# One butterfly level ahead of a block inverse, and a new order of the first loads, in a convolution and FFN kernel

## The chip, the cores and the metric

The kernel runs on one core of a Trainium2 chip. Its engines work side by side, each through its own list of instructions in order: TensorE (PE, with its weight loads as PEld), VectorE (DVE), ScalarE (ACT), GpSimd (POOL) and SyncE (SP), which here issues nearly all DMAs. They meet at semaphores. The metric is the device time of one launch in microseconds (us). Six runs of the kernel before took 351.58 to 353.56 us, with a median of 353.37 us.

## The reference

Two layers, each run twice, over x of 2048 rows and 512 channels (bf16). Layer A is a long convolution with gates; layer B is a gated FFN of width 1792.

```python
def _A_ref(q, k, v, shift_k, ssm_k, ssm_D):          # S = 2048
    k_shift = sum of 4 shifted copies of k, each times a tap per channel
    kv = k_shift * v
    y = irfft(rfft(pad(kv, 2S)) * rfft(pad(ssm_k, 2S)))[:S].astype(bfloat16)
    y = y + kv * ssm_D
    return q * y
def _B_ref(x, w_gate, w_up, w_down):
    return (silu(x @ w_gate) * (x @ w_up)) @ w_down
x = A_q
x = x + _A_ref(layernorm(x), k, v, ...)
x = x + _B_ref(layernorm(x), ...)
x = x + _A_ref(layernorm(x), k, v, ...)
x = x + _B_ref(layernorm(x), ...)
```

The convolved sequence y doesn't depend on x, so it is computed once and used by both A layers. The term with ssm_D is folded into the filter's first row.

## The kernel before

**Tiling.** The 2048 rows are cut into four blocks of 512, and a block into four residues r of 128 rows (row 4p + r lies on partition p). The convolution is done by blocks in the frequency domain. A block's spectrum has four slots with a real and an imaginary part of 128x512 each. Forward transforms are matmuls with the tables `fwd` (14 blocks of 128x128), computed on the chip; inverse transforms use the tables `inv`, which are `fwd` transposed by two DMA transposes (L966). `G[j]` is the spectrum of filter block j, `X[i]` that of block i of k_shift * v; `product(i, j)` (L619) adds X[i] * G[j] into `Z[i + j]`, and an inverse turns Z[k] into `Y[k]`, four rows of 128x512.

**Stages.** The first block has a path of its own. `load_h`, `load_k`, `load_v`, `load_x` (L356 to L394) and `load_weights` bring in filter, k, v, q and the three weights. `transpose_h` (L471) turns the filter, `half` (L429) and `butterfly` (L441) make G[0], `transpose_k` and `shift_mul` make k_shift * v in v's buffer `vt`, `direct` (L454) makes X[0] by 32 matmuls without a butterfly, `product` is called slot by slot, and `inverse_direct` (L686) makes Y[0]. In `inverse_direct` every one of the four output rows sums over all four slots and both parts: 4 x 4 x 2 = 32 matmuls of 128x512 into four PSUM buffers, which ACT then copies to Y (L701). The later blocks use `inverse` (L673) instead: two butterfly levels on VectorE and 8 matmuls.

`prologue(0, 0, 0, True)` (L779) follows: the normalised rows n are multiplied by y and added to x (L797, L799), `ln_stats` (L704) takes the statistics of the new rows on VectorE and raises them to -1/2 on POOL (L714), `normalise` writes z (L764), TensorE transposes z into `ptz` (L811), and ACT copies that to zT (L813), which the first FFN unit multiplies with the weights. With `on_pe=False`, as in all later prologues, DMA transposes make zT.

`ffn` (L820) runs 16 units: four blocks, two layers, two halves of 256 rows. A unit has 14 column tiles of w_gate and of w_up in four groups (`GROUPS`); ACT evacuates both (L854, L858), VectorE multiplies them into ht (L861), and w_down is accumulated into `pd` (L874). In some units x is put into pd first, by a matmul with the identity (L833). Convolution work of later blocks, in `conv(c)`, is laid between the units' matmuls.

**Order.** A planner, the class `Plan`, writes out each engine's instructions. Every operation is added with an engine, a cost, the buffers it reads and writes and, if wished, a latency, a due time and operations that come before it (`after`). `dues` works due times back from those that follow, `forward` then simulates the engines and takes, on each, the ready operation by start and due time. Rings such as "pf" (four PSUM buffers), "pd" and "pc" (two each), "v" (one buffer) and "ks" (two) say how many buffers rotate. The constants at the head of the file (`T0`, `DUR`, `STRETCH`, `SLK`) feed the due times only. On the chip an instruction waits for the data and buffers it uses, not for what `after` names. Eight semaphores serve the DMAs in turn, so that a DMA also waits for the eighth before it.

The lines that set SyncE's order of the first loads:

```python
    k0 = load_k(0, -69)
    v0 = load_v(0, -59, after=[k0])
    x0 = load_x(0, -58, after=[v0])
    wg = load_weights("g", -57, after=[x0])
    for n in range(2):
        ...
        tabs = add("SP", 2.2, ... dma_start_transpose(out=inv.t[:, sl, :], ...), due=-56.8, after=[wg])
    load_h(1, "SP", -56.5, after=[tabs])
    load_k(1, -56.4, after=[tabs])
    load_weights("u", -56, after=[tabs])
    load_weights("d", -55, after=[tabs])
```

Block 1's v, added later as `v1 = load_v(1, ...)`, takes the one buffer of ring "v" that block 0 used. Its product with k_shift is on VectorE too (L513), out of the copies ks that ACT makes (L512).

Of the kernel before, what the change touches and what calls it, by code (L numbers as in the profile page):

```python
# [19 lines left out]
SLK = 25.89  # L20
# [3 lines left out]
ASL = -144.04  # L24
# [4 lines left out]
HSL = 57.15  # L29
# [3 lines left out]
TINY = 0.2  # L33
Z_DUE = -45
X_PE = lambda l, c, h: (l, c, h) in {(0, 0, 0), (1, 2, 0)}
RINGS = {}
T0, FLOOR = 48.85, 3.32
DUR = [32.03, 59.44, 73.66, 74.27, 18.69, 11.93, 40.53, 46.32, 9.45, 36.19, 57.12, 39.57, 69.48, 86.77, 41.93, 24.18]
STRETCH = {1: {'PE': 13.87, 'DVE': 6.22, 'ACT': 7.89, 'POOL': 860.46, 'SP': 1855.74}, 2: {'PE': 5.7, 'DVE': 2.02, 'ACT': 0.72, 'POOL': 0.5, 'SP': 3.41}, 3: {'PE': 16.83, 'DVE': 2.04, 'ACT': 0.66, 'POOL': 0.59, 'SP': 6.47}}
# [26 lines left out]
class Plan:  # L66
# [50 lines left out]
    def dues(self, stretch, floor, units, back):  # L117

        nxt = {}
        for o in reversed(self.ops):  # L120
            d = 1e9 if o.fixed is None else o.fixed
            if isinstance(d, tuple):
                unit, share, shift, kind = d
                d = units[unit][0] + share * units[unit][1] + shift - back.get(kind, 0.0)
            for s in o.succs:
                d = min(d, s.due - o.cost - self.gap(o, s, s.preds[o]))
            if o.conv:
                d = min(d, nxt.get(o.eng, 1e9) - o.cost * stretch[o.grp][o.eng])
                nxt[o.eng] = d
                d = max(d, floor)  # L130
            o.due = d - o.sl

# [138 lines left out]
def kernel(  # L271
# [84 lines left out]
    def load_h(b, eng="SP", due=None, after=()):  # L356
        hn[b] = new("s8" if b == 1 else "h", "hn", [P, KD, L], parts=1)
        q = nc.sync if eng == "SP" else nc.scalar
        return add(eng, 0.55, lambda: q.dma_start(out=hn[b].t[:], in_=h3[:, :, b * L:(b + 1) * L]), w=[hn[b]], lat=(3.9, 10.0)[b] if b < 2 else 6.0, due=due, after=after)

    def load_k(b, due=None, after=()):
        if b == 0:
            kn[b] = new("s8", "kn", [P, R, D])
            return add("SP", 0.5, lambda: nc.sync.dma_start(out=kn[b].t[:], in_=k_t[:, b]), w=[kn[b]], lat=3.9, due=due)
        kT[b] = new("s8" if b == 1 else "k", "kTb", [P, KD, PADL + L])
        add("SP", 2.2, lambda: nc.sync.dma_start_transpose(out=kT[b].t[:], in_=k3[b * L - PADL:(b + 1) * L]),
            w=[kT[b]], lat=12.0 if b == 1 else 8.0, due=due, after=after)

    def transpose_k(b, ring, engs):
# [3 lines left out]
        for dt in range(KD):  # L373
# [5 lines left out]
            add("PE", pe(R, P), go, r=[kn[b], ident], w=[pt])  # L379
# [4 lines left out]
            else:  # L384
                add("DVE", tt1(D), lambda src=src, dst=dst: nc.vector.tensor_copy(out=dst(), in_=src()), r=[pt],
                    w=[(kT[b], (dt,))])

    def load_v(b, due=None, after=()):
        vt[b] = new("v", "vt", [P, R, D], parts=R)
        return add("SP", 0.6, lambda: nc.sync.dma_start(out=vt[b].t[:], in_=v_t[:, b]), w=[vt[b]], lat=4.5 if b else 5.3, due=due, after=after)  # L390

    def load_x(c, due=None, after=()):
        xs[c] = new("x", "xc", [P, R, D], parts=R + 2)
        return add("SP", 0.7, lambda: nc.sync.dma_start(out=xs[c].t[:], in_=q_t[:, c]), w=[xs[c]], lat=4.5 if c else 6.3, due=due, after=after)  # L394
# [17 lines left out]
    def spectrum(name):  # L412
        return new("s8", name, [P, 4, 2, D], parts=8)
# [105 lines left out]
    def by_residue(rows, ev, scale, ring, engs, conv):  # L519

        for r in range(R):
            for part, f in enumerate(("C", "nS")):
                ps = new(ring, "ps", [P, D], F32)
                add("PE", pe(1), lambda ps=ps, f=f, r=r: mm(ps.t[:], [(fT(f, r), rows.t[:, r, :])]),
                    r=[(rows, (r,)), fwd], w=[ps], conv=conv, dest=ev)
# [160 lines left out]
    def inverse_direct(k, slots_order):  # L686
# [13 lines left out]
        for r in range(R):  # L700
            add("ACT", act(D), lambda r=r: nc.scalar.copy(out=y.t[:, r, :], in_=pss[r].t[:]), r=[pss[r]], w=[(y, (r,))])  # L701


    def ln_stats(c, rows):  # L704
# [9 lines left out]
        add("POOL", PW, lambda: nc.gpsimd.tensor_tensor(out=rstd.t[:], in0=ve.t[:], in1=nhalf.t[:].to_broadcast((P, n)),  # L714
# [64 lines left out]
    def prologue(layer, c, h, on_pe=False):  # L779
# [16 lines left out]
        for o, i in enumerate(rows):  # L796
            dve(D, lambda o=o, i=i: nc.vector.tensor_mul(out=n.t[:, o, :], in0=n.t[:, o, :], in1=y.t[:, i, :]),  # L797
                [(y, (i,))], [(n, (o,))])
            dve(D, lambda o=o, i=i: nc.vector.tensor_add(out=x.t[:, i, :], in0=x.t[:, i, :], in1=n.t[:, o, :]),  # L799
                [(n, (o,))], [(x, (i,))])  # L800
        st = ln_stats(c, rows)
        stats = plan.ops[-2]
        done = []
        for o, i in enumerate(rows):
# [8 lines left out]
            add("ACT", act(D), lambda pt=pt, o=o: nc.scalar.copy(out=zT.t[:, :, o, :], in_=pt.t[:]), r=[pt], w=[(zT, (o,))], due=Z_DUE)  # L813
# [149 lines left out]
    wg = load_weights("g", -57, after=[x0])  # L963
    for n in range(2):
        sl = slice(n * NI, (n + 1) * NI)
        tabs = add("SP", 2.2, lambda sl=sl: nc.sync.dma_start_transpose(  # L966
            out=inv.t[:, sl, :], in_=fwd.t[:, sl, :].rearrange("p k f -> p (k f)")), r=[fwd], w=[(inv, (n,))], lat=8.0, due=-56.8,
            after=[wg])
    load_h(1, "SP", -56.5, after=[tabs])
    load_k(1, -56.4, after=[tabs])  # L970
    load_weights("u", -56, after=[tabs])
    load_weights("d", -55, after=[tabs])
    hs = transpose_h(0, "pf", (0, 2, 1, 3), False, ("DVE", "ACT"), drow)
    ev = spectrum("ev")
    G[0] = H[0] = spectrum("G0")
    half(hs, ev, "ac", 2.0 / N, "pf", ("ACT", "DVE"), False, -60)
# [20 lines left out]
    transpose_k(0, "pc", ("ACT", "DVE"))  # L997
    shift_mul(0, "pf", False, due=-49)
    normed[0, 0, 0] = apply_norm(0, 0, on_act=True, due=-47)
    butterfly(ev, G[0], 0, False)  # L1000
    X[0] = spectrum("X0")
    direct(vt[0], X[0], "pf", ("ACT", "ACT"), (0,))
    half(hs, ev, "bd", 2.0 / N, "pf", ("ACT", "ACT"), False)
    butterfly(ev, G[0], 1, False)
    direct(vt[0], X[0], "pf", ("ACT", "ACT"), (2, 1, 3))
# [6 lines left out]
    inverse_direct(0, (0, 2, 1, 3))  # L1012
# [89 lines left out]
```

## Time and profile before

| what | value |
|---|---|
| profiled execution, whole | 351.21 us |
| its span, first to last instruction | 349.4 us |
| granted TensorE clock | 1.00 |
| median of six runs | 353.37 us |
| L697, inverse matmuls of 128x512 | 32 |
| first and last start of L697 | 19.6 and 41.2 us |
| z L764, first start | 34.27 us |
| first FFN matmul (pf, L334) | 36.83 us |
| v of block 1: issue, time to landing | 21.74, 11.7 us |

The profile's rows read as follows. A row of the groups or the timeline has the engine, the line of the source, the operation, the buffer written and those read, and the shape; "x4" counts instructions. In the chain of waits each step is what released the one after it, or what stood before it on its engine, so it leads back from the last instruction. In the rows by stretch the busy us of each engine stand with the number of instructions in brackets, then the granted clock, the mean busy share of the 16 DMA engines, which can pass 1 where packets overlap, and GB/s. Times count from the start of the span. A few per cent of the matmul records are missing in the trace, so their counts run a little short.

### The profile page before, as it was taken

The page shows a single profiled execution, that of the slowest core. Times are in us where ns is not written, and L with a number is a line of the kernel's source. Part 1 is how long each engine was busy: PE and PEld are TensorE (multiplying, and loading weights), DVE is VectorE, ACT ScalarE, POOL GpSimd, SP SyncE. Part 2 cuts the span into 40 slices and gives each one's busy share as a digit, 9 for nine tenths or more (in the row PEclk, how much of TensorE's full clock was granted, in tenths as well). Part 3 has the DMA queues.
Part 4 walks back from the last instruction along what each step waited for, and adds up shares of the span by engine and source line. Part 5 has one row for each costly group of instructions (what it writes and reads, how often), then busy time and mean ns, then how long its engine had stood idle before and what let it go on. Part 6 is the DMA issues. An engine that isn't in the chain of part 4 may idle for free.

```text
span 349.4 us, 6596 instructions
## 1 busy us (share of the span) xinstructions
PE 339.9 (97%) x2597; PEld 249.0 (71%) x2625; DVE 276.6 (79%) x466; ACT 259.0 (74%) x508; POOL 38.1 (11%) x46
## 2 busy tenths in 40 slices
PE   7997999999999999999999999999999999999996
PEld 6655876858588685858586777758586877777684
DVE  6885989999998997899999999999997523643120
ACT  6986996757779994938896989859983756548460
POOL 4100010211120100201212001101001000100000
PEclk9999999999999999999999999999999999999999
DMA  7999211010152106320113030120101110000201
GB/s 255 307 331 350 52 60 32 0 32 0 34 118 64 30 13 141 101 51 2 31 33 76 17 102 20 38 54 0 33 30 28 35 32 0 17 17 1 62 0 30
DMA packets 42073, 22.96 MB, mean 66 GB/s; under 512 B 33845, under 2 KB 39866, under 8 KB 42042
## 3 DMA queue, kind: packets, MB, share of 16 engines
q1 hardware_dynamic: 41370, 21.95, 23.8%
q10 hardware_dynamic: 672, 0.59, 0.6%
q8 instruction: 20, 0.33, 0.4%
q14 instruction: 11, 0.09, 0.1%
HBM read 12.33 MB, written 2.10 MB: 41 GB/s over the span
## 4 chain that ended last, share of the span: by engine, by line
PE 77%; DVE 14%; DMA 5%; ACT 2%; issue 1%; DVEq 0%
PE pf L334 46%; PE pd L874 23%; PE ps L334 5%; DMA vt<-in_A_v_dram 3%; PE ps L462 2%; DVE ht L861 2%; DVE bnst L709 1%; DVE t L649 1%; DMA hn<-in_A_ssm_k_dram 1%; DVE t L657 1%; DVE t L645 1%; DVE Z L659 1%; DVE ka L600 1%; DVE Z L654 1%; DVE m L532 1%
## 5 line engine op out<-in xcount | busy, mean ns | idle before, releaser
L334 PE MATMUL pf<-zT,wg_sb 128*128 128x256 bf16 x896 | 116.1, 273 | 0.2
L334 PE MATMUL pf<-zT,wu_sb 128*128 128x256 bf16 x896 | 116.1, 273 | 0.1
L334 PEld LDWEIGHTS <-wg_sb 128*128 128x128 bf16 x896 | 87.5, 98 | 17.5 <-issue 1.1
L874 PE MATMUL pd<-wd_sb,ht 128*128 128x512 bf16 (+1 forms) x445 | 97.8, 372 | 1.1 <-issue 0.2
L334 PEld LDWEIGHTS <-wu_sb 128*128 128x128 bf16 x896 | 87.7, 98 | 13.0 <-issue 0.2
L854 ACT ACTIVATE sg<-pf 128x512 bf16<-128x512 f32 x112 | 67.6, 605 | 15.6 <-PE pf L334 14.1
L874 PEld LDWEIGHTS <-ht 128*128 128x128 bf16 x462 | 44.9, 98 | 48.0 <-DVE ht L861 1.2
L858 ACT CAST ht<-pf 128x512 bf16<-128x512 f32 x112 | 66.1, 590 | 15.0 <-PE pf L334 14.3
L861 DVE TENSOR_TENSOR ht<-ht,sg 128x1024 bf16<-128x1024 bf16 (+1 forms) x64 | 39.3, 618 | 24.8 <-ACT ht L858 24.8
L714 POOL TENSOR_TENSOR rstd<-ve,nhalf 128x2 f32<-128x2 f32 x24 | 26.2, 1093 | 215.4 <-DVE ve L712 206.2
L910 ACT CAST dn<-pd 128x512 bf16<-128x512 f32 x26 | 14.1, 597 | 35.0 <-PE pd L874 35.0
L709 DVE BATCH_NORM_STATS2 bnst<-xc 128x6 f32<-128x512 bf16 x48 | 31.0, 685 | 0.7
L913 DVE TENSOR_TENSOR xc<-xc,dn 128x1024 bf16<-128x1024 bf16 x13 | 8.9, 687 | 17.1 <-ACT dn L910 17.1
L645 DVE TENSOR_TENSOR t<-X,G 128x2048 bf16<-128x2048 bf16 x18 | 21.9, 1217 | 0.1
L649 DVE TENSOR_TENSOR t<-X,G 128x2048 bf16<-128x2048 bf16 x18 | 21.9, 1216 | 0.0
L423 ACT ACTIVATE X<-ps 128x512 bf16<-128x512 f32 x32 | 18.2, 613 | 0.2 <-PE ps L462 0.2
L659 DVE TENSOR_TENSOR Z<-Z,t 128x2048 bf16<-128x2048 bf16 x12 | 14.7, 1222 | 0.2
L657 DVE TENSOR_TENSOR t<-t,t 128x2048 bf16<-128x2048 bf16 x12 | 14.7, 1221 | 0.2
L740 POOL TENSOR_TENSOR rstd<-ve,nhalf 128x2 f32<-128x2 f32 x8 | 7.6, 956 | 64.2 <-ACT ve L738 64.2
L786 DVE TENSOR_TENSOR n<-n,Yk 128x1024 bf16<-128x1024 bf16 x15 | 10.3, 690 | 5.4 <-ACT n L759 4.1
L423 ACT ACTIVATE H<-ps 128x512 bf16<-128x512 f32 x24 | 12.9, 610 | 2.1 <-PE ps L334 2.1
L734 ACT ACTIVATE jk<-xc,nm 128x512 bf16<-128x512 bf16 x16 | 11.5, 721 | 0.3
(105 smaller groups left out, 319.3 us busy)
## 6 DMA issues: line engine op xcount, KB each, us to landing
vt<-in_A_v_dram SPq DMA_DIRECT2D x4, 512.0 KB, 6.6
xc<-in_A_q_dram SPq DMA_DIRECT2D x4, 512.0 KB, 7.4
out_dram<-xc SPq DMA_DIRECT2D x15, 128.0 KB, 1.8
wg_sb<-in_B_w_gate_dram SPq DMA_DIRECT2D x1, 1792.0 KB, 12.3
wu_sb<-in_B_w_up_dram SPq DMA_DIRECT2D x1, 1792.0 KB, 7.8
wd_sb<-in_B_w_down_dram SPq DMA_DIRECT2D x1, 1792.0 KB, 13.6
hn<-in_A_ssm_k_dram SPq DMA_DIRECT2D x3, 512.0 KB, 7.2
hn<-in_A_ssm_k_dram ACTq DMA_DIRECT2D x1, 512.0 KB, 4.1
```

The source lines that it names most:

```text
L334: nc.tensor.matmul(o, lhsT=lhsT, rhs=rhs, start=(n == 0), stop=(n == len(terms) - 1))
L423: add("ACT", act(D), lambda: nc.scalar.activation(out=view(), in_=ps.t[:], func=ACT.Copy, scale=scale), r=[ps], w=[(buf, keys)], conv=conv)
L645: dve(n * D, lambda t1=t1, part=part: nc.vector.tensor_mul(out=t1.t[:], in0=x.t[:, sl, 0, :], in1=g.t[:, sl, part, :]), [(x, key(slots, (0 ...
L649: dve(n * D, lambda t2=t2, part=part: nc.vector.tensor_mul(out=t2.t[:], in0=x.t[:, sl, 1, :], in1=g.t[:, sl, 1 - part, :]), [(x, key(slots ...
L657: dve(n * D, lambda t1=t1, t2=t2, comb=comb: nc.vector.tensor_tensor(out=t1.t[:], in0=t1.t[:], in1=t2.t[:], op=comb), [t2], [t1], conv=conv)
L659: dve(n * D, lambda t1=t1, part=part: nc.vector.tensor_add(out=z.t[:, sl, part, :], in0=z.t[:, sl, part, :], in1=t1.t[:]), [t1], [zk], con ...
L709: add("DVE", 0.6, lambda st=st, i=i: nc.vector.bn_stats(out=st.t[:], in_=xs[c].t[:, i, :]), r=[(xs[c], (i,))], w=[st])
L714: add("POOL", PW, lambda: nc.gpsimd.tensor_tensor(out=rstd.t[:], in0=ve.t[:], in1=nhalf.t[:].to_broadcast((P, n)), op=ALU.pow), r=[ve, nha ...
L854: add("ACT", act(D), lambda ps=ps, o=o, sg=sg: nc.scalar.activation(out=sg.t[:, o:o + 2, :], in_=ps.t[:], func=ACT.Silu), r=[ps], w=[(sg, ...
L858: add("ACT", act(D), lambda ps=ps, o=o, ht=ht: nc.scalar.copy(out=ht.t[:, o:o + 2, :], in_=ps.t[:]), r=[ps], w=[(ht, (o // 2,))], due=(uni ...
L861: dve(n * W, lambda sg=sg, ht=ht: nc.vector.tensor_mul(out=ht.t[:], in0=ht.t[:], in1=sg.t[:]), [sg], [ht], due=(unit, k / pairs, 0.0, "h"))
L874: nc.tensor.matmul((pds[o] if not cs.start else pds[HP]).t[:, cs], lhsT=ht.t[:, q, o * P:(o + 1) * P], rhs=wt["d"].t[:, ft, cs], start=(ft ...
```

## The change

Block 0's inverse is made by a new function `inverse_half`. VectorE forms sums and differences of the slots s and s + 2 (four operations of 128x1024), and each output row then sums over two slots and two parts: 16 matmuls of 128x512 in place of 32. Row 0 of y is not copied to SBUF before its first use: VectorE multiplies straight from PSUM, and ACT copies the row for later use. In that prologue the second row's zT is evacuated on VectorE instead of ACT.

The load of filter block 1 is put ahead of w_gate. The two table transposes get, besides w_gate, the first transposes of k0 as predecessor in the planner, and are added after them. The planner's estimates of several loads and many due-time constants change, and 27 operations get an extra shift of their due time (`SHIFTS`). `X0` and `H0` select the paths that the kernel before had ("direct", "half"); only `I0` selects a new one.

```diff
-SLK = 25.89
+SLK = 25.57
-ASL = -144.04
+ASL = -167.89
-HSL = 57.15
+HSL = 49.11
+SHIFTS = {8: -168.0, 9: -2.0, 32: -48.0, 36: -20.0, 48: -11.0, ... }
+X0, H0, I0 = 'direct', 'half', 'half'
-T0, FLOOR = 48.85, 3.32
+T0, FLOOR = 25.95, -54.39
...
+        for n, d in SHIFTS.items():
+            self.ops[n].due += d
...
-        return add(eng, 0.55, ..., lat=(3.9, 10.0)[b] if b < 2 else 6.0, due=due, after=after)
+        return add(eng, 0.55, ..., lat=(3.9, 8.0)[b] if b < 2 else 6.0, due=due, after=after)
...
-            add("PE", pe(R, P), go, r=[kn[b], ident], w=[pt])
+            o = add("PE", pe(R, P), go, r=[kn[b], ident], w=[pt])
+            k_in = o if dt == 0 else k_in
...
-        for r in range(R):
+        fresh[k] = pss
+        evacuate_y(k, range(1, R))
+    def evacuate_y(k, rows):
+        y, pss = Y[k], fresh[k]
+        for r in rows:
             add("ACT", act(D), lambda r=r: nc.scalar.copy(out=y.t[:, r, :], in_=pss[r].t[:]), r=[pss[r]], w=[(y, (r,))])
+    def inverse_half(k, pairs):
+        y, z = new_y(k), Z[k]
+        m = spectrum("m")
+        pss = [new(("pd", "pd", "pf", "pf")[r], "ps", [P, D], F32) for r in range(R)]
+        count = [0] * R
+        for s in pairs:
+            for slot, op in ((s, ALU.add), (s + 2, ALU.subtract)):
+                dve(2 * D, lambda s=s, slot=slot, op=op: nc.vector.tensor_tensor(
+                    out=m.t[:, slot], in0=z.t[:, s], in1=z.t[:, s + 2], op=op), ...)
+            for r in range(R) if s == pairs[-1] else (0, 2, 1, 3):
+                for part in (0, 1):
+                    f, q, slot = next((f, q, t) for f, q, t, pt in INV_TERMS[r] if t % 2 == s and pt == part)
+                    count[r] += 1
+                    add("PE", pe(1), ... nc.tensor.matmul(pss[r].t[:], lhsT=iT(f, q), rhs=m.t[:, slot, part], ...),
+                        r=[(m, (2 * slot + part,)), inv], w=[pss[r]])
+        fresh[k] = pss
+        evacuate_y(k, range(1, R))
...
-            dve(D, lambda o=o, i=i: nc.vector.tensor_mul(out=n.t[:, o, :], in0=n.t[:, o, :], in1=y.t[:, i, :]),
-                [(y, (i,))], [(n, (o,))])
+            if i == 0:
+                ps = fresh[c][0]
+                dve(D, lambda: nc.vector.tensor_mul(out=n.t[:, 0, :], in0=n.t[:, 0, :], in1=ps.t[:]), [ps], [(n, (0,))], one=True)
+                evacuate_y(c, (0,))
+            else:
+                dve(D, lambda o=o, i=i: nc.vector.tensor_mul(out=n.t[:, o, :], in0=n.t[:, o, :], in1=y.t[:, i, :]),
+                    [(y, (i,))], [(n, (o,))])
...
-            add("ACT", act(D), lambda pt=pt, o=o: nc.scalar.copy(out=zT.t[:, :, o, :], in_=pt.t[:]), ...)
+            if o:
+                add("DVE", tt1(D), lambda pt=pt, o=o: nc.vector.tensor_copy(out=zT.t[:, :, o, :], in_=pt.t[:]), ...)
+            else:
+                add("ACT", act(D), lambda pt=pt, o=o: nc.scalar.copy(out=zT.t[:, :, o, :], in_=pt.t[:]), ...)
...
-    wg = load_weights("g", -57, after=[x0])
-    for n in range(2):
-        tabs = add("SP", 2.2, ... dma_start_transpose(out=inv.t[:, sl, :], ...), lat=8.0, due=-56.8, after=[wg])
-    load_h(1, "SP", -56.5, after=[tabs])
-    load_k(1, -56.4, after=[tabs])
-    load_weights("u", -56, after=[tabs])
-    load_weights("d", -55, after=[tabs])
+    h1 = load_h(1, "SP", -57.5, after=[x0])
+    wg = load_weights("g", -57, after=[h1])
...
-    transpose_k(0, "pc", ("ACT", "DVE"))
+    k_in = transpose_k(0, "pc", ("ACT", "DVE"))
+    for n in range(2):
+        tabs = add("SP", 4.0, ... dma_start_transpose(out=inv.t[:, sl, :], ...), lat=5.5, due=-56.8, after=[wg, k_in])
+    load_k(1, -56.4, after=[tabs])
+    load_weights("u", -56, after=[tabs])
+    load_weights("d", -55, after=[tabs])
...
-    inverse_direct(0, (0, 2, 1, 3))
+    if I0 == "half":
+        inverse_half(0, (0, 1))
+    else:
+        inverse_direct(0, (0, 2, 1, 3))
```

## The prediction

> **What bounds the kernel now.** I first read the busy shares and the waits of TensorE, then the chain of waits in order of time, then SyncE's queue and the DMA rate by stretches. Busy shares, and all waits of TensorE over the whole span (total us, times, longest):
>
> ```profile
> PE 339.9 (97%) x2597; PEld 249.0 (71%) x2625; DVE 276.6 (79%) x466; ACT 259.0 (74%) x508; POOL 38.1 (11%) x46
> ...
> PE ptz L811 <- DVE z L764: 2.3, 1, 2.3
> PE wm L1068 <- POOL ident masks.py:199: 1.7, 1, 1.7
> PE pt L481 <- DMA hn<-in_A_ssm_k_dram: 0.3, 1, 0.3
> PE pd L874 <- issue: 0.2, 1, 0.2
> ```
>
> TensorE waits once for something that the change can touch: 2.3 us ahead of ptz, the transposes that feed the first FFN unit. Restricted to 36 us and later, the waits hold only the last line, 0.2 us. So from the first FFN matmul (36.83) to the last matmul (345.6) TensorE never waits, and the end is that start plus TensorE's remaining work. The chain around the wait (start, us, what):
>
> ```profile
> 21.74 11.73 DMA vt<-in_A_v_dram
> 33.59 0.76 DVE vt L513 x2
> 34.35 0.33 DVE z L764
> 34.73 0.72 PE ptz L811 x8
> 35.45 0.89 PE ps L334 x16
> 36.35 0.43 PE ps L697 x2
> 36.78 0.05 issue
> 36.83 1.91 PE pf L334 x16
> ```
>
> The wait is no arithmetic. Block 1 of v (v1) lands at 33.46. VectorE takes its instructions in order, and the two products vt L513 that need v1 stand ahead of z L764, so the first normalised rows wait for v1. Its DMA starts only when v0's buffer is free (21.74, X0's last matmul) and then lies behind the weights on SyncE's queue (first two rows: issues of SyncE; then each stretch with engines' busy us, clock, DMA share and GB/s):
>
> ```profile
> 18.66 0.51 SPq L401 DMA_DIRECT2D wd_sb<-in_B_w_down_dram  x1
> 21.74 3.10 SPq L390 DMA_DIRECT2D vt<-in_A_v_dram  x1
> ...
> 12.50:15.00 2.50, 2.45 (x14) 1.08 (x12) 2.50 (x5) 2.38 (x7) 0.44 (x1) 1.00 1.32 131
> 15.00:19.50 4.50, 4.50 (x22) 2.04 (x21) 3.48 (x7) 4.50 (x10) 0.80 (x1) 1.00 1.28 309
> 19.50:20.50 1.00, 1.00 (x7) 0.42 (x5) 0.81 (x2) 1.00 (x4) 0.00 (x0) 1.00 0.49 104
> 20.50:33.50 13.00, 11.80 (x101) 7.33 (x101) 8.00 (x20) 9.71 (x18) 0.69 (x1) 1.00 1.05 376
> ```
>
> From issue and time to landing: wg 15.1, the two inv transposes 15.8 and 16.7, h1 before 22.0 (its transposes start), wu 25.8, wd 32.3, v1 33.46. Plain loads run at 376 GB/s. Before a group of transposing DMAs the rate falls to 131 for 2.5 us (1.6 us lost), after it to 104 for 1.0 us (0.7 lost). Inside the group, with h1 between transposes, nothing is lost (309).
>
> **The change, part by part.**
>
> *Matmuls.* The inverse of block 0 goes from 32 matmuls of 128x512 to 16. Two take 0.43 us (L697 in the chain), so 16 x 0.215 = 3.44 us leaves TensorE. Where it leaves decides. In the built instruction streams, before has 29 inverse matmuls ahead of the first FFN matmul and 3 behind; after has all 16 ahead, and moves the two identity matmuls that put x into pd ahead too. Ahead of the start: 29 - 16 - 2 = 11, so -2.4 us; behind it 3 + 2 = 5, so -1.07 us. The 2.4 us only lengthens the wait for v1; if v1 came early it would be earned. The 1.07 us is earned anyway.
>
> *VectorE.* Four sums of 128x1024 are added; two such take 1.29 us (L634), so 2.58 us. Row 0's product now reads PSUM: 0.68 us (L516) for 0.42 (L797), +0.26. In before the last product Z ends at 25.39 and row 0's statistics at 29.92. With ACT's evacuation unhooked from row 0 the stretch 26.71 to 29.92 becomes 25.39 + 2.58 + 3.21 + 0.26 = 31.44; POOL's power takes 0.69, so z could start at 32.1. Before, it starts at 34.27. The 2.8 us are therefore hidden by v1, and cost up to nothing unless v1 comes before 31.3.
>
> *SyncE's queue.* The condition that holds the tables until k0 is read exists in the planner only; the table transposes carry no wait for k0's readers. What changes on the chip is the order. Before: wg, inv, inv, h1, k1, wu, wd, v1. After: h1, wg, inv, k1, wd, inv, wu, v1. The bytes ahead of v1 are the same, and v1's release (X0's last matmul) comes 0.2 us earlier, one inverse matmul no longer ahead of it. But the second table transpose now stands alone between two weight loads: one more entry and exit of a transposing group. No row shows a lone one. **Bounds:** from 0 (no new loss) to 1.6 + 0.7 = 2.3 us. A loss on entry is an average over 16 engines; it includes waiting for the last of them, whose lag v1 pays in before as well. I take half, +1.1 us: v1 at 34.6. [...] The rows give 309 within the group and 131 and 104 at its edges; the rows decide.
>
> h1 earlier and k1 ahead of wu give TensorE its block-1 work sooner; that work is ahead of the wait, and its gain is swallowed by it. inv's second half lands near 27 for matmuls that come at about 26; up to 1 us of waiting, hidden by v1 as well. The new inverse then ends near 32.3, before z.
>
> *From v1 to the first FFN matmul.* Before: 36.83 - 33.46 = 3.37 us, the last 1.3 of it filler on TensorE. After: vt, vt, z, z on VectorE as before; ACT has ks, ks and one row of y ahead of zT row 0, and VectorE has two vt ahead of zT row 1 (0.69 us, as L385). Added up by the rows (ACT: 0.65 us to its first ks, 3 x 0.59 and 0.59 for zT; VectorE: 2.35 us to its copy, then 0.69), both are done 3.0 us after landing; 3.2 with the handover, -0.17.
>
> *After the start.* Before filled the first FFN groups with the 5 moved matmuls. After runs six groups (0.87 us each) straight into four PSUM buffers, while ACT, held behind zT, still has two sums, two squares and a row of y (about 3.5 us) among its first two evacuations. Bounds 0 to 1.0 us of TensorE waiting; I take 0.5, since four buffers cover 3.5 us.
>
> **Sum:** v1 +1.1, handover -0.17, work behind the start -1.07, evacuation +0.5: **+0.4 us**. The profiled execution took 351.21 us (span 349.4 plus 1.8 around it), 2.2 under the median of the runs, 353.37, which range from 351.58; the difference of 0.4 is carried to the median: 353.8.
>
> All other edits (shifts of due times, planner durations) reorder later work. There TensorE has no wait in before, so reordering cannot gain more than 0.2 us and can lose some; I take nothing.
>
> **The rivals.**
>
> *A, the sum above (0.45).* v1 still ends the wait. Its own bounds: v1 +0.4 to +2.0, the other terms together -1.2 to -0.3: about -0.7 to +1.5, so 352.7 to 354.9.
>
> *B, faster (0.32): v1 stops being the last.* If it lands by 31.3 (0.76 for the two vt ahead of z), VectorE's chain sets z at 32.1: -2.15 on z, -0.17, -1.07, +0.5 = -2.9 us. Landing at 32.5 gives -0.96 - 0.17 - 1.07 + 0.5 = -1.7. Middle -2.2, 351.2. For it: h1 is no longer issued after both tables (12.46 in before), so the 1.6 us lost at 12.5 to 15 may shrink, and all TensorE work ahead is 2.4 us shorter. Against it: the same bytes stand ahead of v1, at a rate that is already 376.
>
> *C, slower (0.23): TensorE cools in a longer wait.* TensorE runs out of work at 32.41 in before (31.80 + 0.61), with 1.3 us of filler still kept for after ptz. After: 32.4 + 1.3 - 2.4 = 31.3, or 32.3 with the wait for inv. ptz comes 1.27 after v1, at 35.9: idle 3.6 to 4.6 us, where before had 2.33. The trace shows a cold start only at the beginning: the 23 warm-up matmuls take 2.63 us, 0.11 each, against 0.056 for equal ones later (L378); after the 2.33 us wait ptz runs at full pace, and the granted clock is 1.00 throughout. [...] By the row the wait costs only itself[...].
>
> That the change does nothing it says is only true of the "hold", and is in A.
>
> **Chances and range.** Under 0.3% (1.06 us) a measurement of this kernel can't tell from no change. A gives 0.30 within it, 0.10 slower, 0.05 faster; B faster, C slower. Faster 0.37, same 0.30, slower 0.33. The range runs from B's far end (-2.9) to C with v1 0.4 us later still (+2.5): 350.4 to 355.9.
>
> **What would show it.** Right: in after, z L798 waits for the DMA of vt, landing at 34 to 35.6; a dip of the DMA rate shortly before 26, around the second table; TensorE's wait before ptz over 3 us; total work of TensorE 3.4 us less. Wrong: v1 landing before 33, ptz waiting for VectorE's chain alone (B), or the first FFN matmuls at twice 109 ns (C). Waits of TensorE after 50 us would show that the new due times, which I cost at nothing, matter.

## The result and the profile after

After: 350.79 us (median of 34 runs, 349.43 to 352.48). Before, run beside it: 351.95 us (69 runs, 351.06 to 355.17). The ratio is 0.9957, with an interval of 0.9945 to 0.9968: 1.5 us faster by the ratio, 1.2 by the medians, where 0.4 us slower was forecast.

Executions of before fall into two groups, near 351.5 and near 353.4 us, and the mean granted clock of TensorE tells them apart: 0.998 to 1.000 in one, 0.993 to 0.995 in the other. Of 172 runs of before made beside the experiments, 91 are at 0.998 or more (medians 351.4 to 351.8 beside each group of kernels) and 81 below it (353.4 to 353.6); a few runs lie in between. The profile of after, whose mean is 0.995, has the clock at 0.50 for one stretch of 3.41 us of its 349.2 (below), so the second group will be called the *cooled* executions. After has them too, 18 of 34, but close together: 351.17 cooled, 350.28 otherwise. The profile of before that the prediction used was not cooled (351.21 us); the profile of after was (351.01 us, span 349.2).

The busy line of after's page:

```profile
PE 338.3 (97%) x2582; PEld 247.8 (71%) x2608; DVE 280.2 (80%) x471; ACT 259.5 (74%) x507; POOL 39.1 (11%) x46
```

TensorE is busy 1.6 us less, not 3.4: about 1.5 us of the difference are matmuls at a clock of 0.50, shown below. Its first four waits over the whole span (total us, times, longest):

```profile
PE ptz L850 <- ACT ks L518: 1.9, 1, 1.9
PE wm L1135 <- POOL ident masks.py:199: 1.7, 1, 1.7
PE ps L731 <- DMA inv<-fwd: 1.1, 1, 1.1
PE pf L338 <- ACT zT L855: 0.8, 1, 0.8
```

The chain of after around the wait (start, us, what):

```profile
22.55 10.70 DMA vt<-in_A_v_dram
...
33.34 0.44 DVE vt L519
...
33.86 0.36 ACT ks L518
...
34.34 0.59 ACT ks L518
34.93 0.49 ACT Yk L715
35.42 0.50 ACT zT L855
...
35.96 6.88 PE pf L338 x48
```

V1 still ends the wait ahead of ptz, though the wait's row names the copy ks: VectorE, which writes z, sat idle for 1.79 us until v1 landed. It landed at 33.25: neither at the forecast 34 to 35.6 nor before 33. From there to the first FFN matmul it takes 2.7 us instead of 3.37, now through ScalarE. Those matmuls are cold, as the timeline of TensorE in after shows (start, us, group, idle before it):

```profile
35.96 1.86 PE L338 MATMUL pf<-zT,wg_sb 128*128 128x256 bf16 x8 [0.76 <-ACT zT L855]
37.62 1.72 PE L338 MATMUL pf<-zT,wu_sb 128*128 128x256 bf16 x8
39.18 1.04 PE L338 MATMUL pf<-zT,wg_sb 128*128 128x256 bf16 x8
```

And by stretches (length, busy us of the five engines, granted clock, DMA share, GB/s), the clock is 0.50 for the 3 us from 36:

```profile
33.50:36.00 2.50, 0.76 (x9) 0.59 (x10) 2.50 (x8) 2.14 (x5) 0.00 (x0) 0.92 1.34 160
36.00:39.00 3.00, 3.00 (x15) 2.08 (x15) 2.97 (x4) 2.94 (x9) 0.00 (x0) 0.50 0.49 112
39.00:42.00 3.00, 3.00 (x29) 2.69 (x28) 2.96 (x5) 2.68 (x8) 0.80 (x1) 1.00 0.00 0
```

Eight matmuls take 1.86 us where eight equal ones take 1.04 from 39.18 on. The forecast kept this for its slower rival, and it happened in half of the executions of the kernel that became faster.

All profiled executions can be split in the same way: start to first FFN matmul, from there to the end of the last matmul, and 3.4 us behind it. The table takes the three points from each trace; "v1" is when 15 of the 16 DMA engines had delivered it, and when the last had (- where another load was put behind v1). The medians are those of all runs of the kernel, while each landing is that of one profiled execution.

```
kernel                v1 15/16      first FFN   to last   span    median
                      engines       matmul      matmul            us
before                32.34  33.47    36.83     309.19    349.4   351.95
before_again          33.59  34.60    39.51     309.20    352.1   351.97
before_warm           33.55  34.22    37.59     309.97    351.0   352.76
before_h1             31.48  32.62    35.98     309.23    348.6   350.79
before_half           33.33  34.36    38.08     307.87    349.3   352.42
before_v1               -             34.68     309.20    347.3   349.13
before_h1_v1            -             34.28     309.23    346.9   348.85
after                 31.75  33.25    35.96     309.88    349.2   350.79
after_tables          32.76  33.36    36.07     309.93    349.4   350.51
after_h1back          33.31  33.85    36.56     308.98    348.9   351.51
after_direct          31.91  33.07    36.81     309.28    349.5   351.45
after_warm            31.40  32.87    35.64     310.14    349.2   350.93
after_wide            33.01  33.06    35.77     309.00    348.2   350.17
after_v1                -             35.01     308.71    347.1   348.75
after_v1_tables         -             34.20     308.72    346.3   348.00
after_v1_tables_act     -             33.67     312.81    349.9   350.70
```

The four profiles of before's order of loads with v1 late on the queue (the first three rows and before_half) have v1 at 33.47, 34.60, 34.22 and 34.36: the one that the forecast stood on is the earliest of them. The four of after's order (after, after_direct, after_warm, after_wide) lie at 32.87 to 33.25.

### The profile page after: what moved, and what is told of

Its sections match the earlier page's. It is cut to its first block, busy times and chain, and to the rows that moved or that the text cites. A ratio compares the mean times of both kernels' runs of the same rounds, so it can differ in the third digit from the quotient of the medians.

```text
span 349.2 us, 6568 instructions
## 1 busy us (share of the span) xinstructions
PE 338.3 (97%) x2582; PEld 247.8 (71%) x2608; DVE 280.2 (80%) x471; ACT 259.5 (74%) x507; POOL 39.1 (11%) x46
## 4 chain that ended last, share of the span: by engine, by line
PE 66%; DVE 20%; ACT 6%; DMA 5%; issue 2%; SPq 0%; DVEq 0%; ACTq 0%
PE pf L338 40%; PE pd L916 18%; PE ps L338 5%; DMA vt<-in_A_v_dram 3%; DVE ht L903 2%; DVE bnst L743 2%; DVE t L655 2%; PE ps L468 2%; DVE t L651 2%; DVE m L538 2%; DVE t L663 2%; DVE Z L665 1%; DMA kn<-in_A_k_dram 1%; ACT ht L900 1%; DVE ka L606 1%
## 5 line engine op out<-in xcount | busy, mean ns | idle before, releaser
L748 POOL TENSOR_TENSOR rstd<-ve,nhalf 128x2 f32<-128x2 f32 x24 | 27.5, 1148 | 219.5 <-DVE ve L746 205.7
L955 DVE TENSOR_TENSOR xc<-xc,dn 128x1024 bf16<-128x1024 bf16 x13 | 8.9, 687 | 15.4 <-ACT dn L952 15.4
L665 DVE TENSOR_TENSOR Z<-Z,t 128x2048 bf16<-128x2048 bf16 x12 | 14.7, 1221 | 0.2
L774 POOL TENSOR_TENSOR rstd<-ve,nhalf 128x2 f32<-128x2 f32 x8 | 7.4, 921 | 59.0 <-ACT ve L772 59.0
```

The lines of the kernel that those rows point to most:

```text
L665: dve(n * D, lambda t1=t1, part=part: nc.vector.tensor_add(out=z.t[:, sl, part, :], in0=z.t[:, sl, part, :], in1=t1.t[:]), [t1], [zk], con ...
L748: add("POOL", pw, lambda: nc.gpsimd.tensor_tensor(out=rstd.t[:], in0=ve.t[:], in1=nhalf.t[:].to_broadcast((P, n)), op=ALU.pow), r=[ve, nha ...
```

## Experiments

The diffs are cut to what differs from the parent; `behind(a, b)` moves one operation directly behind another in the planned order, and nothing else moves. Each kernel's runs stand beside runs of before made with them; the ratio is to these.

**Two groups and the cold clock.** `before_again` is the kernel before, unchanged. `before_warm`, `after_warm` (38 and 36 dummy matmuls of 128x128) and `after_wide` (9 of 128x512) put work on TensorE just ahead of ptz:

```diff
+            if o in self.ahead:
+                self.ahead[o]()
...
+        plan.ahead[ptz[0][0]] = lambda: warm("pf", place[ptz[0][1]], 36)
```

> The kernel before, unchanged, to see the granted TensorE clock of each of its runs; they fall in two groups, near 351.4 and near 353.3 us. Theory 1 (the wait ahead of ptz lets TensorE cool in some executions): the runs near 353.3 show a mean clock of about 0.995 (3.4 us at half rate in 350), those near 351.4 a clock of 1.00. Theory 2 (the landing of v1 alone makes the difference): the clock is 1.00 in both groups.

> The kernel before with 38 small matmuls (128x128, into the PSUM buffer that ptz takes next) put on TensorE just ahead of ptz; they fill about 2.1 us of its 2.3 us wait and are not part of the computation. Theory 1: clock 1.00 in every run, the group near 353.3 disappears, median 351.4. Theory 2: both groups stay, median as the kernel before.

> The changed kernel with 36 such matmuls just ahead of ptz, 2.0 us. Theory 1: clock 1.00 in every run, first FFN matmuls at 109 ns each instead of 214, median near 350.2, the time of those runs of the changed kernel that kept their clock (350.3; those at 0.995: 351.2). Theory 2: nothing gained, 350.8, since the landing of v1 sets the start either way.

> The changed kernel with nine dummy matmuls of 128x512 just ahead of ptz (about 1.9 us of work by the 0.215 us each of L731), so that TensorE does not cool in the wait for v1; results are not used. The 36 small dummies of the earlier run did the same, but a transposing DMA of kc took 2.5 us instead of 1.26 near 226 us, with one instruction packet in the same stretch, and a later wait of 1.3 us for zT ate the gain. Theory 1 (the cold start costs about 1.1 us and the later wait came from the moved instruction fetch): 18 added instructions instead of 72, no 1.3 us wait for zT, median about 350.0, all granted clocks at 0.998 or more. Rival (an earlier start always runs into that later wait, because the transposes there are due at a fixed time): the wait of about 1.3 us returns and the median stays at 350.9.

Measured: before_again 351.97, ratio 1.0005 [0.9986, 1.0024]: 11 runs at 0.998 or more (median 351.63) and 11 cooled (353.48). Its profile is a cooled one, and shows what goes with it. TensorE's wait in it:

```profile
PE ptz L811 <- DVE z L764: 3.4, 1, 3.4
```

V1 landed at 34.60, 1.1 us later than in the profile of before, and the first FFN matmul came 2.7 us later: 1.1 from v1, the rest from cold work between (ptz took 0.99 us for 0.72, the next 16 matmuls 1.91 for 1.06).

With dummies all 52 runs have a clock of 0.998 to 1.000, so the cold clock goes with idle time. The traces also show which idle time goes with it. In the four cooled profiles (after, before_again, after_tables, after_v1_tables_act) the clock stands at 0.50 for one stretch of 3.41 us, which starts 9, 9, 9 and 11 such lengths after the point where the record of the clock begins (4.9 us in after). If a span is divided on this grid, the stretch just ahead of the cold one holds 1.11, 0.09, 0.72 and 1.28 us of matmuls; every other stretch up to the one in which the last matmul ends, in all 16 profiles, holds 1.7 us or more, and the clock stays at 1.00 behind it. After and after_h1back have the same two waits, 1.9 and 0.8 us. In after one stretch takes in the whole first wait and half of the second, and the next is cold:

```profile
32.19:35.60 3.41, 1.11 (x10) 0.45 (x8) 2.26 (x7) 1.74 (x4) 0.14 (x1) 1.00 1.27 229
35.60:39.01 3.41, 3.05 (x15) 2.22 (x16) 3.38 (x5) 3.35 (x10) 0.00 (x0) 0.50 0.54 122
```

In after_h1back the border of two stretches, 34.14, lies within the first wait, and the clock stays at 1.00:

```profile
30.73:34.14 3.41, 2.49 (x14) 0.94 (x10) 1.58 (x6) 1.70 (x4) 0.69 (x1) 1.00 1.02 386
34.14:37.55 3.41, 1.72 (x18) 1.43 (x19) 3.41 (x9) 3.10 (x8) 0.00 (x0) 1.00 1.31 200
```

The grid lies elsewhere in each profile (its first point is at 4.9 to 8.4 us), which may be why after cooled in 18 of its 34 runs and not in the others (not tested).

The medians with dummies were 352.76 (ratio 1.0005 [0.999, 1.002]), 350.93 (0.9969 [0.9954, 0.9984]) and 350.17 (0.9931 [0.9906, 0.9956]). That before_warm and after_warm gained nothing had another cause. In before_warm v1 also landed late, at 34.22. In after_warm the first FFN matmul is earlier than in after, but a later wait is new (first line). It is for a transpose zT that stands on SyncE's queue behind four transposing DMAs of kc; one of these took 2.50 us instead of 1.26, and the DMA packets from 219 to 230 us hold an instruction packet. In after the same four take 5.14 us, and there is no such packet. The wait in after_warm:

```profile
PE pf L341 <- DMA zT<-z: 1.4, 2, 1.3
```

SyncE's queue in after_warm:

```profile
221.40 6.38 SPq L613 DMA_TRANSPOSE kc<-ka  x4
227.89 2.51 SPq L830 DMA_TRANSPOSE zT<-z  x2
```

The instruction queue from 219 to 230 us in after_warm (packets, MB, share of 16 engines):

```profile
q8 instruction: 1, 0.02, 0.9%
```

SyncE's queue in after:

```profile
222.67 5.14 SPq L610 DMA_TRANSPOSE kc<-ka  x4
227.91 2.51 SPq L827 DMA_TRANSPOSE zT<-z  x2
```

The kc transposes start 1.3 us earlier in after_warm and end at the same time. The packet of after_warm comes at 223.8 us, within this group; those of after nearest to it come at 214.1 and 233.6. So with the 72 added instructions the packet comes at another time. In before_warm the same group took 6.06 us with a packet in it, at 225.0 instead of 233.2, and TensorE waited 0.8 us. after_wide adds 18 instructions; the wait did not come, and its 309.00 against 309.88 prices the cold start of after at 0.9 us. What it leaves, besides the handover to the first FFN matmul (first line), are small waits, among them one for ScalarE's late evacuation of the FFN's PSUM (ht L904):

```profile
PE pf L341 <- ACT zT L859: 0.7, 1, 0.7
PE pd L920 <- DVE ht L907: 0.3, 1, 0.3
PE pf L341 <- ACT ht L904: 0.3, 1, 0.3
```

**The lone table transpose.** `after_tables`: the second table directly behind the first.

```diff
+        first_, second = sorted(inv_op.values(), key=seq.index)
+        behind(second, first_)
```

> The changed kernel with the second table transpose moved up behind the first on SyncE's queue, so that no table stands alone between the weights; nothing else moves. If a lone transposing group costs v1 what the prediction took (1.1 us), v1 lands near 32.4 instead of 33.5 and the time falls by 1 us or more, to about 349.7. If its edges cost v1 nothing, since they only take up what the engines lag behind each other, v1 lands between 33.2 and 33.8 and the time stays at 350.8; TensorE's 1.1 us wait for the table near 25 goes in both cases without showing in the time.

Measured: 350.51, 0.3 us below after; ratio 0.9953 [0.9931, 0.9975]. V1 landed at 33.36 in the profile, as in after (33.25): in these two executions the lone table cost v1 nothing. In the landings of after all 16 engines deliver the table within 25.83 to 26.00, and v1 lands with its last engine, at 33.25, when the other 15 were done at 31.75. Why the table cost that last engine nothing isn't shown. TensorE no longer waits for the table, but all the longer for v1:

```profile
PE ptz L854 <- ACT ks L521: 3.4, 1, 3.4
```

Twelve of its 16 runs are cooled. Compared within the groups it is faster than after, 349.21 against 350.28 uncooled (only four runs) and 350.69 against 351.17 cooled. The medians therefore hide up to 1.1 us, and whether v1 lands earlier in executions that were not profiled isn't shown.

**H1's place.** `before_h1` is before with h1 alone moved ahead of wg; `after_h1back` is after with h1 alone moved back behind the first table.

```diff
+        behind(h1, x0)        # before_h1
+        behind(h1, first_)    # after_h1back
```

> The kernel before with one DMA moved: h1 is issued ahead of wg, as in the changed kernel, instead of between the table transposes and k1. Theory 1 (the executions of before near 353.5 come from an instruction packet on one DMA engine at the entry of the transposing group near 13 us: 0.96 us in the run with span 349.4, 2.16 us in the run with span 352.1, where v1 landed 1.1 us later and TensorE cooled in the longer wait): with h1 ahead, the group is entered about 1.4 us later, the packet is past, v1 lands near 33.4 in every execution, all granted clocks are 0.998 or more, the executions lie within 351 to 352 with a median near 351.4. Rival 1 (the packet meets the group anyway, or h1's place has nothing to do with it): executions at 353 to 354 with a clock of 0.995 remain, median 351.8 to 352.4. Rival 2 (h1 in the gap between transposing DMAs was free, and ahead it costs 1.4 us of v1's time): v1 lands at 34.5 or later, median 352.5 or more.

> The changed kernel with h1 moved back: issued behind the first table transpose and ahead of k1, as in the kernel before, instead of ahead of wg; the new inverse, the lone second table and the rest stay. Theory 1 (h1's place alone carries the gain: with it the kernel before went from 352.9 to 350.8, with executions near 353.4 down from 25 of 47 to 2 of 22): the transposing group is entered near 13 us again, within the instruction packet, executions with a late v1 come back, median 351.8 to 353. Rival (in the changed kernel the new inverse and zT's copy on VectorE carry it, h1 adds little on top): median 350.4 to 351.2, as the changed kernel.

Measured: before_h1 350.79, ratio 0.9956 [0.9939, 0.9972] (before beside it: 352.93): **the same ratio as the whole change**. Cooled are 2 of its 22 runs, against 25 of 47 for before beside it; the others have a median of 350.76, 1.0 us below before's. after_h1back: 351.51, ratio 0.9972 [0.9956, 0.9988], between the ranges of the theory and of the rival. By the ratios 0.5 us of after's 1.5 goes with h1, and the two intervals overlap. The executions above 353 did not come back (highest 352.56). So h1's move alone does as much as the whole change, and without it two thirds are left: the parts don't add up.

What h1's move changes is seen at the entry of the first group of transposing DMAs. The stretches below are of one microsecond each (last column GB/s); the single lines are the instruction queue in the microsecond of its packet. Before, then its packet, which starts at 12.95 us:

```profile
13.00:14.00 1.00, 0.95 (x5) 0.43 (x5) 1.00 (x3) 0.97 (x4) 0.00 (x0) 1.00 2.53 111
14.00:15.00 1.00, 1.00 (x6) 0.44 (x5) 1.00 (x3) 0.91 (x4) 0.44 (x1) 1.00 0.19 26
15.00:16.00 1.00, 1.00 (x6) 0.48 (x5) 0.74 (x2) 1.00 (x3) 0.80 (x1) 1.00 1.28 287
```

```profile
q8 instruction: 1, 0.02, 6.1%
```

Before_again, its packet starting at 13.26 us:

```profile
13.00:14.00 1.00, 1.00 (x5) 0.42 (x5) 1.00 (x3) 0.97 (x4) 0.00 (x0) 1.00 1.54 128
14.00:15.00 1.00, 1.00 (x5) 0.39 (x4) 0.84 (x2) 0.91 (x5) 0.37 (x1) 1.00 2.66 97
15.00:16.00 1.00, 0.95 (x5) 0.38 (x4) 0.45 (x1) 1.00 (x4) 0.42 (x1) 1.00 0.05 5
```

```profile
q8 instruction: 1, 0.02, 13.4%
```

Before_h1, its packet starting at 13.77 us, but the full rate lasting to 14:

```profile
13.00:14.00 1.00, 0.95 (x5) 0.38 (x4) 1.00 (x3) 0.93 (x4) 0.00 (x0) 1.00 1.05 396
14.00:15.00 1.00, 1.00 (x7) 0.41 (x6) 1.00 (x3) 0.76 (x2) 0.57 (x1) 1.00 1.86 173
15.00:16.00 1.00, 1.00 (x6) 0.48 (x5) 0.95 (x3) 1.00 (x4) 0.58 (x1) 1.00 0.74 122
```

```profile
q8 instruction: 1, 0.02, 5.6%
```

After_h1back:

```profile
13.00:14.00 1.00, 1.00 (x7) 0.41 (x6) 1.00 (x3) 0.60 (x3) 0.23 (x1) 1.00 2.35 104
14.00:15.00 1.00, 1.00 (x6) 0.48 (x5) 0.48 (x1) 0.81 (x2) 1.00 (x1) 1.00 0.17 16
```

Against 376 GB/s before loses (376-111 + 376-26)/376 = 1.6 us at the entry. In before_again the packet takes 13.4% of 16 engines' microsecond, 2.1 us instead of 1.0, and the loss is 2.4 us; the packet ends at 15.4, and from 15 to 16 us all 16 engines together move 5 GB/s. With h1 ahead the group is entered a microsecond later, the packet is over at 14.7, and the loss is 1.2 us. Moved back, 104 and 16 GB/s return.

The other traces bear this out. In before_again, before_warm, before_half and before_v1 the first table lands 2.3 to 2.5 us behind the last of wg; in before, after_h1back and the ten profiles with h1 ahead, 0.65 to 0.85. In the four the packet is over at 15.0 to 15.9 us, in the twelve at 13.6 to 14.7. In before_warm one engine alone was late: 15 of 16 delivered the table at 15.18, the last at 16.77, with the packet from 14.7 to 15.9. So with before's order a late packet and a late table come together in some executions, and the profile of before was not one of them; that the one causes the other was not tested by itself. Against that profile v1 is 0.85 us earlier in before_h1, of which the entry explains 0.4; the rest is not traced.

**The new inverse.** `before_half` is before with the new inverse alone; `after_direct` is after with the old one. Both are planned anew, and in after_direct the numbers of `SHIFTS` follow their operations.

```diff
-    inverse_direct(0, (0, 2, 1, 3))
+    inverse_half(0, (0, 1))                            # before_half
-X0, H0, I0 = 'direct', 'half', 'half'
+X0, H0, I0 = 'direct', 'half', 'direct'               # after_direct
```

> The kernel before with the new inverse of block 0 alone: 16 matmuls and four sums on VectorE instead of 32 matmuls; loads, tables, row 0 and zT as before. In the built order all 16 matmuls and the two that put x into pd stand ahead of the first FFN matmul. Theory 1 (what leaves TensorE ahead of v1 only lengthens the wait; what leaves behind it, 1.07 us, is earned; the longer wait cools TensorE, about 1.5 us): v1 lands at 33.4 to 34.6 as in before, TensorE waits 3 us or more ahead of ptz, the first FFN matmul starts at 36.2 to 37.2, clock 0.995 in most executions, median 351.2 to 352.6. Rival (3.4 us of work taken from the busiest engine is worth most of it): median 349.5 or less.

> The changed kernel with the inverse of block 0 in its old form, 32 matmuls and no sums on VectorE; the loads, the table's place and row 0 from PSUM stay. Theory 1 (work ahead of the wait for v1 is swallowed by the wait): TensorE is busier by 3.4 us ahead of ptz, which fills the wait of 1.9 us (no cooling) and delays the first FFN matmul by 0.6 to 1.2 us to about 36.6 to 37.2; total 350.9 to 351.9, that is 0 to 1 us above the changed kernel. Rival (the matmuls removed from an engine that is busy 97 per cent are worth their full 3.4 us): median near 354.

Measured: before_half 352.42, ratio 0.999 [0.9972, 1.0008]: nothing. The first FFN matmul came at 38.08, later than expected, with v1 at 34.36. Its four uncooled runs have a median of 350.49, 1.3 us below before's uncooled ones (351.76), close to the 1.3 us that the table shows behind the first FFN matmul (309.19 to 307.87). But 18 of 22 runs are cooled, eight of them with 0.988 to 0.990, about the 0.990 that two stretches of 3.41 us at 0.50 would give (an estimate). after_direct: 351.45, 0.7 us above after, ratio 0.9974 [0.9959, 0.9989], and never cooled: TensorE has no wait ahead of ptz, which the 16 extra matmuls fill. 3.4 us of work on an engine that is 97% busy are worth 0.7 by the medians (the intervals of the two ratios overlap), and 1.2 against after's uncooled runs.

**V1 out of the way.** `after_v1` and `before_v1` issue wu behind v1. `before_h1_v1` adds h1's move to before_v1, `after_v1_tables` the table's move to after_v1, and `after_v1_tables_act` puts one sum and two squares of ScalarE behind the first four evacuations of the FFN.

```diff
+        behind(wu, v1)
```

> The changed kernel with wu issued behind v1 on SyncE's queue instead of ahead of it; nothing else moves. Theory 1 (v1's place on the queue ends the wait): v1 lands near 27.6 to 28.5, z then waits for VectorE's and POOL's statistics (z at about 32.3), ptz at about 33, first FFN matmul at 34.2 to 34.6 instead of 35.96, no cooling, median 348.8 to 349.8. Rival (the last bytes of the queue are needed at the same moment, whichever they are): wu lands at 33.3 on its last DMA engine, the first matmuls of wu wait for it, the start of the second FFN group is at 35.5 or later, and the median is 350.3 to 351.

> The kernel before with wu issued behind v1 on SyncE's queue; nothing else moves. Theory 1 (in the kernel before, too, v1's place on the queue is the bound): v1 lands near 27.5 to 29, ptz no longer waits for it, TensorE's remaining work ahead of the first FFN matmul (done near 32.4 with the wait) then sets the start at 34.3 to 35 instead of 36.83, no cooling, median 349.3 to 350.3, better than the changed kernel. Rival: wu, now last, makes the second FFN group wait, or TensorE's longer inverse sets the start at 36 or later, and the median stays within 0.5 us of 352.

> The kernel before with h1 ahead of wg and v1 ahead of wu: the old inverse with all loads in the best order found. Theory 1 (with v1 out of the way TensorE never runs dry ahead of the first FFN matmul, so its 3.4 us of extra inverse work count there): first FFN matmul near 34.5, as with v1 alone, median 348.8 to 349.4, 0.8 to 1.4 us above the changed kernel with the same order of loads (348.0). Rival (the new inverse is worth nothing even then): median within 0.4 us of 348.0.

> The changed kernel with v1 ahead of wu and the second table transpose directly behind the first. With v1 ahead alone the chain went through the second table (issued 18.02, landed 26.64), TensorE waited 1.1 us for it, and VectorE's chain followed. Theory 1 (the table is now the bound): the table lands near 18 to 19, no wait for inv, row 0's statistics and z about 1 us earlier (z near 32), first FFN matmul near 34.0 to 34.4 instead of 35.0, median 347.8 to 348.3, the fastest so far. Rival (VectorE's sums, which need the last product Z, or wu's landing, bound it at the same time): first FFN matmul at 34.8 or later, median 348.5 to 349.

> The same, and ScalarE takes the first four evacuations of the FFN's PSUM buffers ahead of one sum and two squares for the next rows' statistics, instead of among them. Theory 1 (the evacuations stall TensorE by 0.14 us with v1 ahead, 0.4 in the changed kernel with dummy matmuls): 0.1 to 0.4 us below the kernel without it. Rival (the statistics are then late for the next half's rows): a new wait for ptz or zT near 50 us, and no gain or a loss.

Measured: after_v1 348.75, ratio 0.9889 [0.986, 0.9918]; before_v1 349.13, 0.9896 [0.9868, 0.9925]; before_h1_v1 348.85, 0.9892 [0.9863, 0.9922]; after_v1_tables **348.00, 0.9856 [0.9829, 0.9883]**, the fastest; none cooled. One swap on the queue is worth about 3 us (before beside these: 352.38), twice the whole change. In before_v1 TensorE then has only the first wait, ahead of all work, and a 0.2 us one; in after_v1 the first FFN matmul comes at 35.01, later than expected, since the chain has passed to the lone table, then to VectorE's statistics (chain of waits):

```profile
18.02 8.62 DMA inv<-fwd
26.69 0.39 PE ps L734
...
27.77 0.59 ACT Yk L718
28.38 0.70 DVE n L836
...
32.28 0.82 POOL rstd L751
33.12 0.74 DVE z L801 x2
```

So here the lone table does cost, 0.8 us by the median and by the first FFN matmul. With the loads in the best order all the rest of the change (the inverse, row 0, zT, due times) is worth 348.85 - 348.00 = 0.85 us; both differences rest on five or six runs a kernel, and the intervals of the ratios overlap. The last kernel got slower than its parent: 350.70, ratio 0.9945 [0.9925, 0.9965], 3 of 10 runs cooled. The first FFN matmul is earlier, but on ScalarE the statistics moved back to 37.9 us, and the evacuations of X came behind them at 42.3 instead of 40.4. TensorE waits for X's PSUM until 42.9 (first line of its waits):

```profile
PE ps L341 <- ACT X L432: 2.5, 1, 2.5
```

## Why the prediction was wrong

*What bounds it*: right. V1's landing ends the wait in both kernels, and moving v1 up the queue gives about 3 us in before.

*"I take half, +1.1 us: v1 at 34.6"*: the step that failed. In after v1 landed at 33.25, 0.2 us ahead of before's 33.47 instead of 1.1 behind it. Two things were wrong in the term. The first is what it left out: h1's move counted only as earlier work for TensorE, "its gain is swallowed", and its effect on the entry loss stood in rival B in one sentence, unpriced. By the profiles it brings v1 forward by 0.85 us (before_h1 against before) or 0.6 (after against after_h1back), and the late landings of before seem nearly gone with it (2 of 22 runs cooled). The second is the size of the new loss. The rest of the new order then costs v1 0.4 to 0.6 us (after_h1back against before, after against before_h1), not 1.1; and in the profile of after_tables, without the lone table, v1 lands no earlier. Landings of one order differ by up to 1.1 us between profiles, so these sizes are rough. The edge losses were mean rates of 16 engines, while v1's time is set by the last one (33.25 in after, where 15 of 16 had delivered at 31.75). Two readings beside it were wrong too: "nothing is lost (309)" is 0.8 us in 4.5 at 376 GB/s, and v1 was issued 0.8 us later (22.55), not 0.2 earlier. And rival A narrowed the bounds of 0 to 2.3 us to 0.4 to 2.0 without a reason.

The edges were real in after too: inside, the group of transposing DMAs moves 287 and 291 GB/s (16 to 18 us), and its entry loses 1.4 us (164 and 78 GB/s from 14 to 16 us, against 376).

*"The difference of 0.4 is carried to the median"*: failed as well. From profile to profile the change gives -0.2 us: v1 -0.2, handover from v1 to the first FFN matmul -0.7, behind the start -0.2 without cooling, cooling +0.9. The forecast of +0.4 misses that by 0.6; the other 1.0 to 1.3 us of the miss lie in the executions that the profile of before does not stand for. The median of six, 353.37, lay in before's upper group, and the profile in the lower. What the change does to the share and the height of the upper group, no sum made on one execution could show.

*Handover, -0.17*: right mechanism, mis-sized; -0.65. The same step took 3.36 us in before_h1, and 2.71 in after_tables, after_h1back and after_wide. zT row 1's copy on VectorE took 0.41 us, not 0.69, and ScalarE's operations follow one another at 0.49, not 0.59.

*Behind the start, -1.07 and +0.5*: -0.57 forecast, -0.19 in after_wide, -0.48 in after_v1. The five matmuls left. In after_wide the stall of evacuations was 0.4 us, within its bounds; small waits of 0.2 to 0.3 (ht, zT), where before has one of 0.2, added 0.1 to 0.3. They were costed at nothing, as a part of the new due times, which were not tested alone. Some 0.2 to 0.3 us are not placed.

*Rival C, cooling*: seen, in 18 of 34 runs, at 0.9 us (309.88 against 309.00). The size that the range's upper end, +2.5, gives it is shown by no trace of before. Of the 3.41 us at a clock of 0.50, 3.05 held matmuls, which makes 1.5, and the stall of 0.4 us that after_wide has is absent in after, presumably because ScalarE then has more time for an evacuation (eight matmuls took 1.72 to 1.86 us instead of 1.04); that was not tested. Nor did it take the one idle of 3.6 to 4.6 us that the forecast saw coming: the waits were 1.9 and 0.8 us, and the stretch of the grid ahead of the cold one held 1.11 us of matmuls. And before cooled itself, in 81 of 172 runs, which one uncooled profile hid.

*Rival B's sign* was right, and its remark that h1 may shrink the entry loss; its mechanism was not, since v1 is still the last. Its 351.2 lies near the measured 350.79 by luck.

*What stays open*: whether the lone table costs something in uncooled executions, why the packet takes 2.1 us in the profile of before_again and 1.0 in that of before, why it coincides with a late table in four profiles only, and why after_h1back has no run above 352.56 (in its one profile the table is not late). That late v1 and cooling go together in before rests on one profile of each kind; in before_half v1 was late without cooling. Row 0 from PSUM, zT's copy on VectorE and the new due times were not run alone.

## What to carry to other kernels

Before a sum is made on one profiled execution, look at how the runs are distributed: a change can gain by removing a bad group of executions that the profile never shows. Where a load ends a wait, follow its slowest DMA engine, not the mean rate (v1's came up to 1.5 us behind the other 15), and ask what it stands behind on its queue: here one swap was worth twice the change. When runs fall into groups, compare within them too: equal medians can hide a gain and a greater share of cooled executions. A probe can change more than it is meant to: with 72 added instructions in after_warm an instruction packet came within a group of transposes and TensorE waited 1.3 us for zT, and with 18 in after_wide that wait did not come. Few and large ones were the safer probe here.

## What the runs showed of the hardware

The instruction packets, 16 KB each, took 0.9 to 1.6 us in before and after, and the first one 2.1 us in before_again (13.4% of 16 engines' microsecond). In four profiles the first one ended at 15.0 to 15.9 us, and the first table landed 2.3 to 2.5 us behind wg; in twelve it ended at 13.6 to 14.7, and the table landed 0.65 to 0.85 behind. In after_warm, with a packet at 223.8 us, one transpose of kc took 2.50 us instead of 1.26. The entry of such a group was slow without a packet too: after moves 164 and 78 GB/s from 14 to 16 us instead of 376, its packet having ended at 13.8. A second packet lies between 26 and 34 us, and the last engine of v1 comes up to 1.5 us behind the other 15; that the one causes the other was not tested.

In the four cooled profiles TensorE's clock stood at 0.50 for 3.41 us, behind a stretch of a grid of 3.41 us that held 0.09 to 1.28 us of matmuls; in all 16 profiles it stayed at 1.00 behind those with 1.7 or more. Waits of 1.9 and 0.8 us were thus enough in the profile of after (18 of its 34 runs are cooled), and in that of after_h1back the same two left the clock at 1.00.
